# A linear-attention scan fused with a two-layer network: the first chunks' scores as whole 128-token products

## Chip, cores and metric

One NeuronCore of a Trainium2 chip. The metric is the device time of one execution in microseconds, from its start to its end on the slowest core (here the only one). Three executions of the kernel before were timed. One execution was also recorded by the hardware profiler; the rows below come from that one.

## The reference

For 4 batches, 8 heads, 768 tokens and 48 columns a head, all float32:

```
for t in range(768):
    cur = outer(u * k[t], v[t])
    y[t] = r[t] @ (state + cur)
    state = w[:, None] * state + outer(k[t], v[t])
h = x @ w_in                     x: 3072 tokens x 384 (the heads' y side by side), w_in: 384 x 2048
g = max(h, 0) + alpha * min(h, 0)
out = g @ w_out                  w_out: 2048 x 384
```

The decay w lies between 0.85 and 0.95 and differs by head and column.

## The kernel before, in words

**Chunks and pairs.** The tokens are cut into 6 chunks of L = 128. Heads go in P = 4 pairs: the first head of a pair lies in partitions 0 to 47, the second in 64 to 111, so that both use half of TensorE's rows. Within a chunk the scan becomes products: scores k'r between tokens (k and r scaled by powers of w from the tables W[q], made on VectorE), masked to earlier tokens, with u's share on the diagonal; then the scores times v; plus r times the state that came from earlier chunks.

**Chunk 0** is `first_chunk(q)`, lines 420 to 515, once for each pair. VectorE multiplies r and k by the tables (L431) and takes their product (L519). TensorE sums it with u (L526), ScalarE copies the sums to `cu` (L530). The scores are made in 64-token blocks: the two diagonal blocks (L445) and the cross block from early to late tokens (L449). `base` holds the diagonal blocks: first the identity times `cu` (ScalarE for the first heads, L462; VectorE for the second, L456), then VectorE writes the scores over it where the mask is set (L466). ScalarE copies the cross block to `off` (L470). `out` multiplies with v in two pieces (L480): the first 64 rows of the scores, then the last 64. ScalarE looks at one element between them (L486). The result is split in two parts of reduced precision (`xh`, `xl`: L392, L393, L395, and L381, L382 for the last pair), and some rows are moved by small transfers (L370). `state()` turns k to tokens by rows (`by_tokens`, L298: a product with `spread`, a diagonal matrix of w to the 64th; ScalarE copies it, L302) and multiplies by v (L508); ScalarE scales the result by w to the 64th (L513) into T[q].

**Later chunks** are made by `prepare` and `burst`, lines 537 to 679, pair by pair between the steps of the network, in 64-token halves, with the state handed from half to half (L664). Chunk 1 (`hasty`) also uses `by_tokens` and `diagonal`; from chunk 2 on k by tokens is loaded and scaled on VectorE, and u's sums are made on POOL.

**The network** runs in 96 steps of 128 hidden columns: `m_in` (L689, 9 matmuls: 3 blocks of rows by 3 products of split operands), an epilogue on ScalarE and VectorE (L697, L698, L701, L702), `m_out` (L722, 9 matmuls). Its order is chunk 0 steps 0 to 8, chunk 1 steps 0 to 8, the rest of chunk 0, the rest of chunk 1, then chunks 2 to 5. The weights of each of 16 steps are loaded once (L328) and split by ScalarE and VectorE (L346 to L357; L357, `wl`, is the last).

**What sets the order.** Every piece of work is added to a plan with an engine, an expected duration in us, what it reads and writes, and a rank. `in_order` (lines 95 to 175) runs a list schedule of these numbers; the pieces are issued in the order of their planned starts, so each engine's queue is fixed when the program is built. The first `m_in` has rank 0, by-token products of chunk 0 have rank -40 + q and come after the last product with v, and state products have rank 0.5 q + 0.2.

**Fillers.** `warm` (L233) is a bfloat16 matmul whose result nobody reads. 33 of them open the program; `with_warm` puts some in front of certain pieces, and line 819 to 822 put more into planned gaps of TensorE.

## Time and profile before

| | us |
|---|---|
| median of 3 executions | 505.71 |
| lowest, highest | 504.98, 506.17 |
| profiled execution, its own time | 506.03 |
| its span, first to last instruction | 504.3 |

Busy time of the engines over the span: TensorE 492.1, VectorE 310.8, ScalarE 243.1, POOL 41.9. The mean granted clock of TensorE is 0.975 of full speed. A busy TensorE counts overlapping matmuls once and takes modelled ends, so its share says that it always had something in it, not how fast it went; the granted clock says that. In groups of instructions, the mean duration of one is longer than the distance between two starts, since they overlap.

### The profile page before, as it was taken

What the parts mean: (1) busy time and instruction counts of PE and PEld (TensorE: products, weight loads), DVE (VectorE), ACT (ScalarE), POOL (GpSimd) and SP (SyncE); (2) the same over time, 40 slices, a digit from 0 to 9 for tenths busy, and PEclk for the clock granted to TensorE, in tenths of its full rate; (3) what the DMA queues carried; (4) which work ended last, traced back from release to release, by engine and by line L of the source; (5) the groups of instructions that cost most, each with busy time, mean ns of one, the idle gap of its engine ahead of it and who ended that gap; (6) DMA issues with size and microseconds to landing.
All of it is one profiled execution on the core that took longest, in us unless ns stands there. A gap on an engine that the chain in (4) does not pass through costs nothing.

```text
span 504.3 us, 11838 instructions
## 1 busy us (share of the span) xinstructions
PE 492.1 (98%) x4949; PEld 404.8 (80%) x4949; DVE 310.8 (62%) x522; ACT 243.1 (48%) x565; POOL 41.9 (8%) x48
## 2 busy tenths in 40 slices
PE   8899999899999999999999999999999999999994
PEld 6688888678888888888888888888888887888883
DVE  7553988999988668586476466667544534333331
ACT  4556578566765555355345355444443324422222
POOL 1000001000321101110122020121000000000000
PEclk9856999999999999999999999999999999999999
DMA  7436267646314363141221131312030000100001
GB/s 216 160 89 207 99 199 217 183 164 215 108 50 154 101 199 113 56 147 39 89 74 53 53 130 48 97 57 69 20 96 1 1 1 1 63 0 1 0 1 68
DMA packets 23739, 45.87 MB, mean 91 GB/s; under 512 B 3968, under 2 KB 11264, under 8 KB 23680
## 3 DMA queue, kind: packets, MB, share of 16 engines
q1 hardware_dynamic: 23680, 45.05, 28.6%
q8 instruction: 41, 0.67, 0.6%
q14 instruction: 18, 0.15, 0.1%
HBM read 36.38 MB, written 6.29 MB: 85 GB/s over the span
## 4 chain that ended last, share of the span: by engine, by line
PE 95%; DVE 2%; DMA 1%; issue 1%; SPq 0%; ACT 0%; ACTq 0%
PE bank L689 39%; PE acc L722 39%; PE bank L627 3%; PE bank L637 2%; PE bank L298 2%; PE bank L480 2%; PE bank L606 2%; PE bank L599 2%; PE acc L233 1%; DMA raw<-rk 1%; PE bank L508 1%; PE bank L393 1%; DVE raw L549 0%; PE acc L526 0%; PE bank L526 0%
## 5 line engine op out<-in xcount | busy, mean ns | idle before, releaser
L698 DVE SCALAR_TENSOR_TENSOR g<-bank,alph,g 128x512 f32<-128x512 f32 x96 | 71.9, 749 | 109.8 <-ACT g L697 109.5
L697 ACT ACTIVATE g<-bank 128x512 f32<-128x512 f32 x96 | 57.2, 596 | 141.7 <-PE bank L689 141.5
L689 PE MATMUL bank<-xh,wh 128*128 128x512 f32 x288 | 113.5, 394 | 0.0
L689 PE MATMUL bank<-xh,wl 128*128 128x512 f32 x288 | 112.3, 390 | 0.0
L689 PE MATMUL bank<-xl,wh 128*128 128x512 f32 x288 | 112.1, 389 | 0.0
L702 DVE TENSOR_TENSOR gl<-g,gh 128x512 fp32r<-128x512 f32 x96 | 70.6, 736 | 38.3 <-ACT gh L701 37.6
L701 ACT ACTIVATE gh<-g 128x512 fp32r<-128x512 f32 x96 | 60.5, 630 | 64.2 <-DVE g L698 64.1
L722 PE MATMUL acc<-gh,wh 128*128 128x512 f32 x288 | 83.6, 397 | 1.6 <-ACT gh L701 1.6
L722 PE MATMUL acc<-gl,wh 128*128 128x512 f32 x288 | 81.4, 390 | 0.2 <-DVE gl L702 0.2
L722 PE MATMUL acc<-gh,wl 128*128 128x512 f32 x288 | 81.6, 390 | 0.0
L722 PEld LDWEIGHTS acc<-gl,wh 128*128 128x128 f32 x288 | 53.9, 188 | 11.9 <-DVE gl L702 0.7
L722 PEld LDWEIGHTS acc<-gh,wh 128*128 128x128 f32 x288 | 52.5, 188 | 13.5 <-ACT gh L701 2.4
L689 PEld LDWEIGHTS bank<-xl,wh 128*128 128x128 f32 x288 | 54.2, 188 | 11.3
L689 PEld LDWEIGHTS bank<-xh,wh 128*128 128x128 f32 x288 | 54.2, 188 | 11.4
L722 PEld LDWEIGHTS acc<-gh,wl 128*128 128x128 f32 x288 | 54.0, 188 | 11.5
L689 PEld LDWEIGHTS bank<-xh,wl 128*128 128x128 f32 x288 | 54.2, 188 | 11.1
L560 POOL TENSOR_TENSOR rr<-rr,kk 128x384 f32<-128x384 f32 x16 | 19.8, 1236 | 306.6 <-DMA kk<-vkr 164.7
L571 ACT ACTIVATE base<-ident,cu 128x64 f32<-128x64 f32 x160 | 41.3, 337 | 1.9 <-DVE cu L566 1.8
L382 DVE TENSOR_TENSOR xl<-bank,xh 48x256 fp32r<-48x256 f32 (+1 forms) x66 | 28.4, 430 | 3.8 <-ACT xh L381 2.5
L381 ACT ACTIVATE xh<-bank 48x256 fp32r<-48x256 f32 (+1 forms) x66 | 25.4, 385 | 2.9 <-PE bank L637 1.0
L549 DVE TENSOR_TENSOR raw<-raw,W 112x512 f32<-112x512 f32 x40 | 26.3, 680 | 0.8 <-DMA raw<-rk 0.8
L562 POOL TENSOR_TENSOR rr<-rr,utab 128x384 f32<-128x384 f32 x16 | 19.8, 1239 | 1.3
(107 smaller groups left out, 421.9 us busy)
## 6 DMA issues: line engine op xcount, KB each, us to landing
wraw<-wall SPq DMA_DIRECT2D x16, 768.0 KB, 4.6
raw<-rk SPq DMA_DIRECT2D x46, 224.0 KB, 3.6
v<-vkr SPq DMA_DIRECT2D x24, 192.0 KB, 3.8
kk<-vkr SPq DMA_DIRECT2D x16, 192.0 KB, 3.3
rr<-vkr SPq DMA_DIRECT2D x16, 192.0 KB, 2.5
oT<-o SPq DMA_DIRECT2D x12, 256.0 KB, 2.2
oT<-g SPq DMA_DIRECT2D x6, 256.0 KB, 2.6
xh<-xh SPq DMA_DIRECT2D x36, 32.0 KB, 2.0
```

What stands on the lines that cost most here:

```text
L381: add("ACT", us, lambda: nc.scalar.activation(to(h), view(), AF.Copy), r=[src], w=refs(h), rank=rank)
L382: add("DVE", us + 0.1, lambda: nc.vector.tensor_tensor(out=to(l), in0=view(), in1=to(h), op=ALU.subtract), r=[src] + refs(h), w=refs(l), r ...
L549: add("DVE", 0.72, lambda t=t, tab=tab: nc.vector.tensor_tensor(out=t().rearrange("p b (j t) -> p (b j) t", j=2), in0=t().rearrange("p b ( ...
L560: add("POOL", 1.2, lambda: nc.gpsimd.tensor_tensor(out=rt(), in0=rt(), in1=k(), op=ALU.mult), r=[k] + ([wh[12]] if c == 2 else []), w=[rt] ...
L562: add("POOL", 1.2, lambda: nc.gpsimd.tensor_tensor(out=rt().rearrange("p (g b) e -> p g b e", g=2), in0=rt().rearrange("p (g b) e -> p g b ...
L571: add("ACT", 0.32, lambda g=g, b=b: nc.scalar.activation(base()[:, g, b], ident2(), AF.Copy, scale=cu()[:, g, b:b + 1]), r=[cu, ident2], w ...
L689: nc.tensor.matmul(hp()[:, :], a[i]()[:, k], x[c]()[:, k], start=(k == 0 and j == 0), stop=(k == NK - 1 and j == 2))
L697: add("ACT", 0.6, lambda: nc.scalar.activation(g(), hp()[:, :], AF.Copy), r=[hp], w=[g], rank=n - 100)
L698: add("DVE", 0.75, lambda: nc.vector.scalar_tensor_tensor(out=g(), in0=hp()[:, :], scalar=alph()[:, i:i + 1], in1=g(), op0=ALU.mult, op1=A ...
L701: add("ACT", 0.64, lambda: nc.scalar.activation(gh(), g(), AF.Copy), r=[g], w=[gh], rank=n - 100)
L702: add("DVE", 0.73, lambda: nc.vector.tensor_tensor(out=gl(), in0=g(), in1=gh(), op=ALU.subtract), r=[g, gh], w=[gl], rank=n - 99)
L722: nc.tensor.matmul(banks[k](), a[i]()[:, NK + k], x(), start=(begin and j == 0), stop=(end and j == 2))
```

## The change

Chunk 0: the scores of a head are one product of 128 by 128 tokens instead of three 64-token blocks. Each head's `base` is a tile of its own, whose diagonal is set by ScalarE for both heads, and whose scores VectorE writes under a full 128-token mask (`strict`, cast by POOL). The cross copy, VectorE's diagonal and ScalarE's look are gone. The product with v is one piece over all 128 tokens. `by_tokens` is four transposes and two copies without a scale; the state is scaled once, by w to the 128th (`w128`). Chunk 1 uses tables over 128 tokens too: its k by tokens is transposed, its state update adds without a scale, and ScalarE scales the state at its end. `warm` streams 384 columns instead of 256, with other counts, and the planner's expected durations are changed.

```diff
-BY_DVE = (1,)
+MM = 0.682
+WARM = 0.16
...
-    one, unit, ones = fixed([128, 2], "one"), sb([112, 65], "g", 3), sb([128, 128], "g", 3)
+    one, unit, ones = fixed([128, 2 + P], "one"), sb([112, 65], "g", 3), sb([128, 128], "g", 3)
...
-    spread = sb([112, P, 2, D], "rr", 1)
...
-        nc.tensor.matmul(into()[:, 256:512], x[:, 0:128], x, start=True, stop=True, skip_group_check=True)
+        nc.tensor.matmul(into()[:, 128:512].rearrange("p (a f) -> p a f", a=2), x[:, 0:128],
+                         x[:, None, 0:192].broadcast_to([128, 2, 192]), start=True, stop=True, skip_group_check=True)
 
     def with_warm(n, us, fn, r, w, rank):
 
-        p = add("PE", us + 0.107 * n, lambda: [warm(bank) for _ in range(n)] + [fn()], r=r + [ident] * (n > 0),
-            w=w + [(bank, ("warm", len(plan.pieces)))] * (n > 0), rank=rank)
+        p = add("PE", us + WARM * n, lambda: [warm(bank) for _ in range(n)] + [fn()], r=r + [ident] * (n > 0),
+                w=w + [(bank, ("warm", len(plan.pieces)))] * (n > 0), rank=rank)
         p.warm = n
+        return p
...
+    add("POOL", 0.3, lambda: nc.gpsimd.tensor_copy(strict(), ones()), r=[ones], w=[strict], rank=-60)
...
-    def spreads():
-
+    def small_tables():
         add("ACT", 0.3, lambda: nc.scalar.activation(minus(), ident()[0:112, 0:112], AF.Copy, scale=-1.0), r=[ident],
             w=[minus], rank=-60)
         for m in range(P):
-            add("ACT", 0.3, lambda m=m: nc.scalar.activation(
-                spread()[:, m], ident()[0:112].rearrange("p (g e) -> p g e", g=2)[:, :, 0:D], AF.Copy,
-                scale=W[m]()[:, L:L + 1]), r=[ident, W[m]], w=[(spread, m)], rank=-59 + m)
-
-    def by_tokens(q, k0, k, rank, behind=()):
+            add("ACT", 0.17, lambda m=m: nc.scalar.activation(
+                w128()[:, m:m + 1], W[m]()[:, L:L + 1], AF.Copy, scale=W[m]()[:, L:L + 1]), r=[W[m]], w=[(w128, m)],
+                rank=-39)
+
+    def by_tokens(k0, k, warms, rank, behind=()):
+
         t = psum()
 
-        def product():
+        def turn():
             for b in range(B):
-                nc.tensor.matmul(t()[:, 2 * D * b:2 * D * (b + 1)], k0()[:, b], spread()[:, q].rearrange("p g e -> p (g e)"),
-                                 start=True, stop=True, skip_group_check=True)
-
-        add("PE", 0.77, product, r=[k0, (spread, q)], w=[t], rank=rank).after.update(behind)
-        add("ACT", 0.5, lambda: nc.scalar.activation(
-            k().rearrange("p (g b) e -> p b g e", g=2),
-            t()[:, 0:2 * B * D].rearrange("p (b g e) -> p b g e", b=B, g=2), AF.Copy), r=[t], w=[k], rank=rank)
+                nc.tensor.transpose(t()[:, 112 * b:112 * (b + 1)], k0()[:, b], ident()[0:112, 0:112])
+
+        with_warm(warms, 0.5, turn, r=[k0, ident], w=[t], rank=rank).after.update(behind)
+        for g in range(2):
+            add("ACT", 0.3, lambda g=g: nc.scalar.activation(
+                k()[:, B * g:B * (g + 1)], t()[:, 0:448].rearrange("p (b x) -> p b x", b=B)[:, :, HI * g:HI * g + D],
+                AF.Copy), r=[t], w=[(k, g)], rank=rank)
...
-            for j in range(2):
-                add("ACT", 0.3, lambda m=m, j=j: nc.scalar.activation(
-                    rows()[:, m, HI * j:HI * (j + 1)], W[m]()[:, L - 1:HI - 1:-1], AF.Copy, scale=W[m]()[:, L:L + 1]), r=[W[m]],
-                    w=[(rows, (m, j))], rank=-21).after.update(last_out)
+            add("ACT", 0.36, lambda m=m: nc.scalar.activation(
+                rows()[:, m].rearrange("p (j t) -> p j t", j=2), W[m]()[:, None, L - 1:HI - 1:-1].broadcast_to([112, 2, HI]),
+                AF.Copy, scale=W[m]()[:, L:L + 1]), r=[W[m]], w=[(rows, m)], rank=-21).after.update(last_out)
...
-        lo, hi = slice(0, HI), slice(HI, L)
 
         def scores():
             for b in range(B):
-                at = slice(b * HI, (b + 1) * HI)
                 for g in range(2):
-                    for s in (lo, hi):
-                        nc.tensor.matmul(A[g]()[s, at], k0()[half(g), b, s], r()[half(g), b, s], start=(b == 0),
-                                         stop=(b == B - 1), skip_group_check=True)
+                    nc.tensor.matmul(A[g]()[:, b * L:(b + 1) * L], k0()[half(g), b], r()[half(g), b], start=(b == 0),
+                                     stop=(b == B - 1), skip_group_check=True)
+
+        with_warm(2, 1.05, scores, r=[r, k0], w=A, rank=q - 90)
+        base = [sb([128, B, L], "gl", 3, F32, mv) if q % 2 else sb([128, B, L], "base", 3) for _ in range(2)]
+        for g in range(2):
+            for b in range(B):
+                add("ACT", 0.39, lambda g=g, b=b: nc.scalar.activation(
+                    base[g]()[:, b], ident(), AF.Copy, scale=cu()[:, g, b:b + 1]), r=[cu, ident], w=[(base[g], b)],
+                    rank=-60 + q)
+        for g in range(2):
+            add("DVE", 0.73, lambda g=g: nc.vector.copy_predicated(
+                base[g](), strict()[:, None, :].broadcast_to([128, B, L]),
+                A[g]()[:, :].rearrange("p (b t) -> p b t", b=B)), r=[strict, A[g]], w=[base[g]],
+                rank=10 * q - 76 + g)
+        y = psum()
+
+        def out():
             for b in range(B):
                 for g in range(2):
-                    nc.tensor.matmul(A[g]()[lo, 256 + b * HI:256 + (b + 1) * HI], k0()[half(g), b, lo], r()[half(g), b, hi],
-                                     start=False, stop=(b == B - 1), skip_group_check=True)
-
-        with_warm(3, 0.95, scores, r=[r, k0], w=A, rank=q - 90)
-        base, off = sb([128, 2, B, HI], "base", 3), sb([128, 2, B, HI], "gl", 3, F32, mv)
-        for g in range(2):
-            if g in BY_DVE:
-                add("DVE", 0.42, lambda g=g: nc.vector.tensor_tensor(
-                    out=base()[:, g], in0=ident2()[:, None, :].broadcast_to([128, B, HI]),
-                    in1=cu()[:, g, :, None].broadcast_to([128, B, HI]), op=ALU.mult), r=[cu, ident2],
-                    w=[(base, (g, b)) for b in range(B)], rank=10 * q - 77 + g)
-                continue
-            for b in range(B):
-                add("ACT", 0.32, lambda g=g, b=b: nc.scalar.activation(
-                    base()[:, g, b], ident2(), AF.Copy, scale=cu()[:, g, b:b + 1]), r=[cu, ident2],
-                    w=[(base, (g, b))], rank=-60 + q)
-        for g in range(2):
-            add("DVE", 0.44, lambda g=g: nc.vector.copy_predicated(
-                base()[:, g], strict2()[:, None, :].broadcast_to([128, B, HI]),
-                A[g]()[:, 0:256].rearrange("p (b t) -> p b t", b=B)), r=[strict2, A[g]],
-                w=[(base, (g, b)) for b in range(B)], rank=10 * q - 76 + g)
-            add("ACT", 0.42, lambda g=g: nc.scalar.activation(
-                off()[lo, g].rearrange("p b t -> p (b t)"), A[g]()[lo, 256:512], AF.Copy), r=[A[g]], w=[(off, g)],
-                rank=-59.5 + q)
-        y = psum()
-
-        def out(rows, pieces):
-            for b in range(B):
-                for g in range(2):
-                    to, x = (lo if g == 0 else half(g)), g * B + b
-                    for n, (t, j) in enumerate(pieces):
-                        nc.tensor.matmul(y()[to, b * L + HI * j:b * L + HI * (j + 1)], v().rearrange("p x e -> p (x e)")[
-                            rows, x * D:x * D + to.stop - to.start], t()[rows, g, b], start=(rows == lo and b == n == 0),
-                            stop=(b == B - 1), skip_group_check=True)
-
-        with_warm(2, 0.78, lambda: out(lo, ((base, 0), (off, 1))), r=[v, base, off], w=[y], rank=q - 85)
-
-        add("ACT", 0.2, lambda: nc.scalar.activation(
-            seen_y()[:, 0:2], y()[HI:HI + 1, B * L - 2:B * L], AF.Copy), r=[y], rank=-99)
-        last_out[:] = [add("PE", 0.42, lambda: out(hi, ((base, 1),)), r=[v, base], w=[y], rank=q - 85.1)]
+                    rows, x = (slice(0, HI) if g == 0 else half(g)), g * B + b
+                    nc.tensor.matmul(y()[rows, b * L:(b + 1) * L], v().rearrange("p x e -> p (x e)")[
+                        :, x * D:x * D + rows.stop - rows.start], base[g]()[:, b], start=b == 0,
+                        stop=b == B - 1, skip_group_check=True)
+
+        last_out[:] = [with_warm(3, 0.95, out, r=[v] + base, w=[y], rank=q - 85)]
...
-            by_tokens(q, k0, k, -40 + q, last_out)
+            by_tokens(k0, k, 2, -40 + q, last_out)
...
-            add("PE", 0.47, product, r=[k, v], w=[U], rank=0.5 * q + 0.2)
+            add("PE", 0.75, product, r=[k, v], w=[U], rank=0.5 * q + 0.2)
             T[q] = sb([112, B, D], "T", 9)
-            add("ACT", 0.4, lambda t=T[q]: nc.scalar.activation(t(), u_rows(U, 0), AF.Copy, scale=W[q]()[:, L:L + 1]),
-                r=[U, W[q]], w=[T[q]], rank=0.5 * q + 0.2)
+            add("ACT", 0.4, lambda t=T[q]: nc.scalar.activation(t(), u_rows(U, 0), AF.Copy, scale=w128()[:, q:q + 1]),
+                r=[U, w128], w=[T[q]], rank=0.5 * q + 0.2)
...
-        with_warm(3 if mine != sums else 0, 0.45, c_sum, r=[prod, uw], w=[mine], rank=sum_rank)
+        with_warm(2 if mine != sums else 0, 0.56, c_sum, r=[prod, uw], w=[mine], rank=sum_rank)
...
+        span = L if hasty else HI
+        for t, tab in ((r, lambda: W[q]()[:, None, 0:span]), (k0, lambda: W[q]()[:, None, L - 1:(None if hasty else HI - 1):-1])):
             add("DVE", 0.72, lambda t=t, tab=tab: nc.vector.tensor_tensor(
-                out=t().rearrange("p b (j t) -> p (b j) t", j=2), in0=t().rearrange("p b (j t) -> p (b j) t", j=2),
-                in1=tab().broadcast_to([112, 2 * B, HI]), op=ALU.mult), r=[W[q]], w=[t], rank=at - 2)
+                out=t().rearrange("p b (j t) -> p (b j) t", t=span), in0=t().rearrange("p b (j t) -> p (b j) t", t=span),
+                in1=tab().broadcast_to([112, B * L // span, span]), op=ALU.mult), r=[W[q]], w=[t], rank=at - 2)
...
-            by_tokens(q, k0, k, at - 1.6)
+            by_tokens(k0, k, 0, at - 1.6)
...
-        first = add("PE", (0.7 if before else 0.1) + (0.8 if now else 0.1), run, r=uses, w=writes, rank=at)
+        us = {(1, 1): 3.0 if before and joint else 2.05, (1, 0): 1.8 if before and joint else 1.25, (0, 1): 1.5}
...
-            seen.soon[first] = 0.75
+            seen.soon[first] = 1.7 if joint else 1.05
...
-                    out=t(), in0=of(), scalar=W[q]()[:, L:L + 1], in1=u_rows(A[j], 256), op0=ALU.mult,
-                    op1=ALU.add), r=[A[j], T[q], W[q]], w=[t], rank=at - 0.4)
+                    out=t(), in0=of(), scalar=one()[0:112, 0:1] if c == 1 else W[q]()[:, L:L + 1], in1=u_rows(A[j], 256),
+                    op0=ALU.mult, op1=ALU.add), r=[A[j], T[q], W[q], (one, 0)], w=[t], rank=at - 0.4)
                 T1, T[q] = (t if j == 0 else T1), t
+            if c == 1:
+                add("ACT", 0.4, lambda t=t: nc.scalar.activation(t(), t(), AF.Copy, scale=w128()[:, q:q + 1]), r=[w128],
+                    w=[t], rank=at + 0.5)
...
-            add("PE", 0.7, mm, r=[wh[i], wl[i]] + [(t[c], (kx, p)) for t in (xh, xl) for kx in need for p in range(6)],
+            add("PE", MM, mm, r=[wh[i], wl[i]] + [(t[c], (kx, p)) for t in (xh, xl) for kx in need for p in range(6)],
...
-    add("PE", 7.0, lambda: [warm(bank) for _ in range(33)], r=[ident], w=[(bank, "warm")], rank=-1000)
+    add("PE", 6.7, lambda: [warm(bank) for _ in range(23)], r=[ident], w=[(bank, "warm")], rank=-1000)
...
-            begun = begun or p.rank >= 0 and p.us == 0.7
+            begun = begun or p.us == MM
             gap = 0.0 if last is None else max(0.0, p.start - last - 0.05)
-            if not begun or p.takes and gap > 0.3:
-                fill[p] = int(gap / 0.125), p.takes[0] if begun else bank
+            if gap > 0.25 and (not begun or p.takes):
+                fill[p] = int(gap / 0.17), p.takes[0] if begun else bank
```

The `m_out` pieces take `MM` in place of 0.7 as well, `spreads()` is called as `small_tables()`, and the spacer tile `space` goes.

## Rows read from the trace of the kernel before

**Rows 1.** The page: busy share of TensorE, and its granted clock in 40 slices.
```profile
PE 492.1 (98%) x4949; PEld 404.8 (80%) x4949; DVE 310.8 (62%) x522; ACT 243.1 (48%) x565; POOL 41.9 (8%) x48
...
PEclk9856999999999999999999999999999999999999
```

**Rows 2.** Windows: stretch and length, busy us (instructions) by engine, granted clock, DMA.
```profile
8.00:21.80 13.80, 12.30 (x328) 9.79 (x328) 10.20 (x24) 7.29 (x26) 0.00 (x0) 0.99 0.77 238
21.80:44.50 22.70, 22.70 (x239) 18.86 (x238) 8.18 (x14) 12.00 (x31) 0.00 (x0) 0.50 0.40 122
44.50:102.70 58.20, 56.40 (x783) 45.72 (x781) 51.16 (x81) 37.45 (x88) 2.04 (x2) 0.99 0.58 174
102.70:498.00 395.30, 395.17 (x3569) 326.24 (x3567) 236.40 (x392) 183.10 (x415) 37.55 (x30) 1.00 0.22 69
```

**Rows 3.** The chain of waits in order of time: start, us, what.
```profile
9.14 0.63 PE bank L445 x32
9.77 0.46 PE bank L449 x16
10.23 0.43 PE acc L233 x3
10.66 0.56 PE acc L526 x16
...
16.51 1.11 PE bank L480 x30
...
31.65 1.12 PE bank L393 x2
...
34.27 7.07 PE bank L298 x32
41.34 1.87 PE bank L508 x26
...
44.61 1.32 PE bank L689 x3
...
58.31 0.87 PE bank L298 x8
```

**Rows 4.** Windows of half a microsecond; the granted clock is the third number from the end.
```profile
21.50:22.00 0.50, 0.50 (x12) 0.28 (x7) 0.00 (x0) 0.00 (x0) 0.00 (x0) 0.60 0.00 0
...
45.50:46.00 0.50, 0.50 (x6) 0.37 (x4) 0.00 (x0) 0.50 (x3) 0.00 (x0) 1.00 0.85 167
```

**Rows 5.** Timeline of TensorE: start, us, line, tile, count, [idle before, releaser].
```profile
15.38 0.28 PE L445 MATMUL bank<-raw 48*64 48x64 f32 x3 [0.60 <-issue]
...
21.15 0.71 PE L480 MATMUL bank<-base,v 64*64 64x64 f32 x15 [0.82 <-issue]
```

**Rows 6.** Timeline of TensorE: three transposes and the matmul behind them.
```profile
45.77 0.45 PE L316 MATMUL bank<-ident,g 112*128 112x112 f32 x3
45.99 0.48 PE L689 MATMUL bank<-xh,wh 128*128 128x512 f32 x1
```

**Rows 7.** Groups of ScalarE from 9 to 44.5 us: busy us, mean ns of one.
```profile
L462 ACT ACTIVATE base<-ident,cu 128x64 f32<-128x64 f32 x16 | 4.4, 336 | 0.2
...
L302 ACT ACTIVATE kk<-bank 128x384 f32<-128x384 f32 x4 | 2.0, 490 | 3.9 <-PE bank L298 2.3 <-PE bank L508 1.6
...
L470 ACT ACTIVATE gl<-acc 64x256 f32<-64x256 f32 x4 | 1.3, 367 | 1.3 <-PE acc L449 1.3
```

**Rows 8.** Groups of VectorE from 4.6 to 44.5 us: busy us, mean ns of one.
```profile
L456 DVE TENSOR_TENSOR base<-ident,cu 128x256 f32<-128x256 f32 x4 | 1.7, 418 | 1.5 <-ACT cu L530 1.5
L466 DVE COPY_PREDICATED base<-strict,acc 128x256 f32<-128x256 uint8 x4 | 1.5, 438 | 1.6 <-ACT base L462 1.3 <-ACT gl L470 0.2
```

**Rows 9.** Timelines: the last of step 8's weights (VectorE), its first matmul (TensorE).
```profile
101.76 0.95 DVE L357 TENSOR_TENSOR wl<-wx,wh 128x768 fp32r<-128x768 f32 x1
...
102.69 0.40 PE L689 MATMUL bank<-xh,wh 128*128 128x512 f32 x1
```

More of the change, by code (lines that the diff above doesn't have):

```diff
@@ L310, in half_table @@
         for m in range(P):
[L311 to L314 removed]
+            add("ACT", 0.36, lambda m=m: nc.scalar.activation(
+                rows()[:, m].rearrange("p (j t) -> p j t", j=2), W[m]()[:, None, L - 1:HI - 1:-1].broadcast_to([112, 2, HI]),
+                AF.Copy, scale=W[m]()[:, L:L + 1]), r=[W[m]], w=[(rows, m)], rank=-21).after.update(last_out)
         for m in range(P):
[L316 removed]
+            add("PE", 0.12, lambda m=m: nc.tensor.transpose(
                 pt()[:, 128 * m:128 * m + 112], rows()[:, m], ident()[0:112, 0:112]),
[L318 removed]
+                r=[(rows, m), ident], w=[(pt, m)], rank=-20)
         add("DVE", 0.4, lambda: nc.vector.tensor_copy(
@@ L645, in run @@
                 products()
-        first = add("PE", (0.7 if before else 0.1) + (0.8 if now else 0.1), run, r=uses, w=writes, rank=at)
+        us = {(1, 1): 3.0 if before and joint else 2.05, (1, 0): 1.8 if before and joint else 1.25, (0, 1): 1.5}
+        first = add("PE", us[before is not None, now is not None], run, r=uses, w=writes, rank=at)
         if before:
-            row, col = (HI, L) if joint else (0, L)
+            row, col = (HI, 3 * L) if joint else (0, L)
             seen = add("ACT", 0.2, lambda: nc.scalar.activation(
                 seen_y()[:, 0:2], y[1]()[row:row + 1, col + HI - 1:col + HI + 1], AF.Copy), r=[y[1]], rank=at - 200)
-            seen.soon[first] = 0.75
+            seen.soon[first] = 1.7 if joint else 1.05
             add("PE", 0.3, lambda: through_scores(1), r=[v0, base0], w=y[joint:], rank=at - 200)
@@ L725, in m_out @@
             for k in range(NK):
-                add("PE", 0.7, lambda k=k: [mm(j, (k,)) for j in range(3)], r=[wh[i], wl[i], gh, gl], w=[banks[k]],
+                add("PE", MM, lambda k=k: [mm(j, (k,)) for j in range(3)], r=[wh[i], wl[i], gh, gl], w=[banks[k]],
                     rank=n + MLAG - 0.5)
@@ L729, in m_out @@
             for j in range(3):
-                add("PE", 0.7, lambda j=j: mm(j, range(NK)), r=[wh[i], wl[i], gl if j == 2 else gh], w=banks,
+                add("PE", MM, lambda j=j: mm(j, range(NK)), r=[wh[i], wl[i], gl if j == 2 else gh], w=banks,
                     rank=n + MLAG - 0.5)
```

7 lines of the change are left out of this document (2 added, 5 removed).

## The prediction

> **What bounds the kernel now.** I began with the page: busy shares, then its strip of 40 slices. TensorE is busy for 98% of the span, so time can only be won where TensorE works slowly or on something that need not be done. The strip of the granted clock shows the slow place: full speed everywhere but in slices 2 to 4 [rows 1]. Next came the busy time of each engine by stage [rows 2]. From 21.8 to 44.5 us TensorE is busy all of 22.7 us at a granted clock of 0.50, which is 1.2 GHz of its 2.4, while VectorE has 8.18 us of work and ScalarE 12.00. From 102.7 to 498 us TensorE idles 0.13 us in 395: nothing is to be had there but by removing matmuls. Between these two, from 44.5 to 102.7, TensorE idles 1.8 us and VectorE 7.0.
>
> The chain of waits in order of time says what fills the slow stage: the products with v (L480), the by-token products (L298, 7.07 us for the four pairs), the state products (L508), and then, at 44.61, the first matmul of the feed-forward part (L689) [rows 3]. All of it is TensorE's own queue, one piece after the other. The half-microsecond windows date the clock: it drops inside 21.5 to 22.0 and is back inside 45.5 to 46.0, just after the L689 matmuls start [rows 4]. Ahead of the drop the timeline shows two holes in TensorE that no engine explains, 0.60 and 0.82 us put down to issue, each in the middle of a run of equal matmuls [rows 5].
>
> So the target is one number: the start of the first L689, now 44.6 us. What comes behind it is TensorE bound and moves along with it, if the weights keep up.
>
> **The change on TensorE, pair by pair (four pairs), at the full clock.** Durations are from the chain [rows 3].
> - Scores. Removed: 0.63 + 0.46 = 1.09 us of 64-column products. Added: 8 products (16 instructions) of 128 columns, two row groups side by side. The nearest row has that pattern, the cross block L449: 16 instructions of 64 columns in 0.46; twice the columns gives 0.92. If nothing ran side by side, the price of L298 holds (0.87 / 8 for 96 columns, 0.145 for 128), 2.32 in all; if the four-way pattern of L445 held, 0.63. I take 0.92.
> - Product with v. Removed: 1.11 for the lower half and 0.71 for the upper [rows 3, 5]. Added: 16 instructions of 128 columns over both halves of the tokens. The lower half's row gives 0.037 for 64 columns, so 1.18 in all; the same upper bound of 2.32, lower 0.63.
> - k by tokens. Removed: 0.87. Added: 4 transposes. The trace has transposes in L316: three start at 45.77, and the matmul behind them starts at 45.99, about 0.073 each [rows 6]. Four: 0.30. Upper bound: their single durations end to end, 0.45 each at the worst, 1.8.
> - Filler matmuls. 8 of 256 columns at 0.143 become 9 of 384 columns, 0.215 each if time goes with columns: 1.15 becomes 1.94. The lower bound is that width costs nothing, 0.143 each, or 1.29.
>
> Before: 1.09 + 1.82 + 0.87 + 1.15 = 4.93. After: 0.92 + 1.18 + 0.30 + 1.94 = 4.34. That is 0.6 us a pair, 2.4 in all: small at the full clock. The rest depends on the clock.
>
> The queue up to the first L689 is then 4 x (0.56 for the diagonal sums + 4.34) = 19.6, three subtracting matmuls (L393, 1.12 for two at half clock, so 0.28 each) 0.8, and two state products (L508, 26 instructions in 1.87 at half clock, so 0.58 for 16) 1.2; less 0.4 for the first two fillers, which lie ahead of the first sums: 21.2 us. It starts, as before, when the first product of r and k is there, at about 8.1 us (the first transfers and VectorE's first three passes are untouched). **First L689 at 29.3, 15.3 us earlier.** The kernel of before at full clock would be there at 21.8 + 11.35 = 33.2, so about 11 of the 15 are the clock and 4 are removed work and holes: fewer, longer instructions should meet fewer holes like those of [rows 5].
>
> **Does the clock stay?** In the stage before the drop TensorE spent its time on 64-column products in quarters of the array, 2-column sums, and two holes. Afterwards the products are twice as wide, the filler streams half as many columns again, and planned gaps over 0.25 us are filled. I think it likelier than not that it holds, with no row that proves it.
>
> **ScalarE and VectorE in the same stage.** ScalarE's copies for the diagonal go from 16 of 64 columns to 32 of 128, 0.336 each for 64 [rows 7]; a 384-column copy takes 0.490, so about 0.36 each, some 0.28 apart when back to back: plus 5 us. Removed are the 8 evictions L470 (2.6) and four tiny L486 copies. By tokens it has 8 copies instead of 4, plus 1. From 8 to 44.5 it was busy 19.3 us [rows 2]; about 22 now, of which some 4 (later weights, the half table) can wait. That is 18 us in the 20 between the first sums and 29.3: it fits, with little to spare, and a delay there delays the splits that L689 needs. VectorE loses four L456 (0.418) and doubles the width of eight L466 (0.438) [rows 8]: plus 0.3 on 18.4, in 21 us. What does not fit is the preparation of the second weights, which slides past the first L689.
>
> **From the first L689 on.** Chunk 1's four by-token products save 4 x (0.87 - 0.30) = 2.3 us of TensorE. Its four extra ScalarE scalings of the state (about 0.4 each) have nobody waiting soon, and ScalarE has 20 idle us in that stage [rows 2]: nothing. Its powers over 128 tokens have the same number of elements: nothing. The mask that POOL now casts once more is first read after the first scores, long after POOL is done with its opening work, and the half table's eight copies become four of twice the width on a ScalarE that waits there: nothing for either, a few tenths if the cover went. But this stage runs at the pace of the weights: the last of VectorE's preparation for step 8 ends at 102.71 and that step's matmul starts at 102.69 [rows 9]. With 7.0 idle us of VectorE and up to 2.5 us of second-weight work slid in, I charge 2.3 against the gain (bounds: 0 to 5), so this stage nets zero (minus 2.3 to plus 2.7). The new planner prices (0.682 instead of 0.7 for three matmuls, larger ones for bursts) can reorder pieces; behind 102.7 there are 0.13 idle us to win, and I price that at zero (bounds minus 0.1 to plus 1.5, the size of the idle time already met in the middle stage).
>
> **Sum.** The profiled execution took 506.03 (span 504.3), 0.3 above the median of 505.71. 506.0 - 15.3 = 490.7; against the median **490.4 us**.
>
> **Rivals.**
> *The clock falls late all the same* (about 21.8, as before, or among the transposes). The rest of the queue costs double: at 21.8, 13.7 of 21.2 us are done and 7.5 become 15, first L689 at 36.8, total 498; a fall at 25 gives 494.5. For it: the diagonal sums stay, and transposes and state products are short. Against it: the wider products. The Trainium skill, TensorE: Matmul & The Clock Gate, Part 4 (PE-mode transpose), says that transposes do not count as busy work as matmuls do, and measures about 275 ns for one in a kernel; by that the by-token stage would be where the clock is lost, and the four would take an estimated 1.1 us. No run here shows a clock lost on transposes; L316's starts are closer together than that figure. Chance 0.18.
>
> *The weights hold the middle stage.* If VectorE loses its order as well as its slack, step 8 comes not 15 but 10 us earlier: total 495 to 496. For it: the row pair of [rows 9]. Against: 7 idle us. Chance 0.15.
>
> *Slower: the clock is lost in the first stage.* The start has 23 fillers instead of 33, the sums have 2 instead of 3, and ScalarE's longer copies make TensorE wait. Lost at 9 us, the queue is 0.9 + 2 x 20.3, first L689 at 49.6, total 511. It decides where 8.1 + x + 2 (21.2 - x) = 44.6, x = 5.9: a fall before 14.0 us is slower, one after it faster. Against it: through that stretch the clock of before held [rows 2], with less streamed. Chance 0.08.
>
> *Nothing measurable*: a fall very near 14 us, or several delays that add up to 15. Chance 0.03.
>
> **How the numbers follow.** The forecast has 0.56: 490.4, its own range 486 (fillers at their lower bound, the weights in time) to 494. The range 485 to 500 takes in the late fall and the late weights and leaves the early one out, together with products that do not run side by side (plus 8 to 10). A measurement of this kernel can tell about 0.2%, 1 us, from no change. Faster 0.89 (forecast, late fall, late weights), within 0.2% 0.03, slower 0.08.
>
> **What the profile will show.** Right: no 0.5 window between 20 and 45 us, first L689 between 27 and 32, 16 score instructions in about 0.9 us, transposes near 0.07 apart, the stage from first L689 to step 8 still near 58 us, and the stretch behind it unchanged at 395. Wrong: a half-clock stretch of over 5 us; ScalarE busy without a break to past 30 us with TensorE in fillers; score products at 0.145 an instruction; or step 8's weights at 95 us or later.

## The result and the profile after

The kernel after took 488.32 us in the median (487.33 to 494.74), the kernel before beside it 505.52 (504.98 to 506.17): a ratio of 0.9653, with a 95% interval from 0.9629 to 0.9676. The forecast was 490.4, with 485 to 500 as its range.

Either kernel can lose TensorE's full clock somewhere in its opening stage, the mean granted clock of an execution tells whether it did, and the ratio counts the four executions of before (all of which lost it, by their times) and those of after that kept it. Over all runs of this study the kernel before kept the clock (mean 0.996 or more) in 22 of 53 executions, 493.9 to 496.9 us with a median of 495.6, and lost it in 31, 503.0 to 507.7 with a median of 505.0 (0.969 to 0.979 in the 27 whose clock is on record; the four beside the result are counted by their times). The kernel after kept it in 8 of 9 executions, 487.2 to 491.8 with a median of 488.2, and lost it for long in one, 494.74. So the 17.2 us are two things: 9.9 us (505.5 to 495.6; 9.4 from the median of all 31) for a clock that before loses more often than not, and 7.4 us (495.6 to 488.2), 1.5%, for the kernel at the same clock.

The first profile of after is of that one execution. Its page, on the lines of [rows 1]:

```profile
span 493.0 us, 11246 instructions
PE 483.3 (98%) x4649; PEld 392.4 (80%) x4649; DVE 309.8 (63%) x518; ACT 247.2 (50%) x577; POOL 47.1 (10%) x49
PEclk9589999999999999999999999999999999999999
```

300 matmuls fewer, and a slow place again, but in another slice: earlier than in [rows 1], and shorter. The windows of one microsecond date it (the granted clock is the third number from the end):

```profile
11.00:12.00 1.00, 1.00 (x10) 0.43 (x10) 1.00 (x3) 1.00 (x5) 0.00 (x0) 0.55 1.06 339
...
28.00:29.00 1.00, 1.00 (x14) 0.69 (x14) 0.78 (x3) 0.37 (x1) 0.00 (x0) 0.92 0.11 20
```

The timeline of TensorE has a wait ahead of that fall: the first diagonal sums (L506, before: L526) come at 8.91 after 1.83 idle us, because an input landed late: VectorE waits 1.05 us for a transfer of r and k at 7.47. The first matmul of the network (L675, before: L689) starts at 36.75.

```profile
8.91 0.63 PE L506 MATMUL acc<-uw,g 112*64 112x2 f32 x16 [1.83 <-DVE g L499]
...
36.75 0.50 PE L675 MATMUL bank<-xh,wh 128*128 128x512 f32 x1
```

### The profile page after: what moved, and what is told of

It reads as the page before. It is cut to its first block, busy times and chain, and to the rows that moved or that the text cites. A ratio compares the mean times of both kernels' runs of the same rounds, so it can differ in the third digit from the quotient of the medians.

```text
span 493.0 us, 11246 instructions
## 1 busy us (share of the span) xinstructions
PE 483.3 (98%) x4649; PEld 392.4 (80%) x4649; DVE 309.8 (63%) x518; ACT 247.2 (50%) x577; POOL 47.1 (10%) x49
## 3 DMA queue, kind: packets, MB, share of 16 engines
q1 hardware_dynamic: 23680, 45.05, 29.3%
## 4 chain that ended last, share of the span: by engine, by line
PE 88%; DVE 5%; DMA 3%; ACT 2%; SPq 1%; issue 0%; DVEq 0%; ACTq 0%
PE acc L708 39%; PE bank L675 38%; PE bank L609 2%; DMA raw<-rk 2%; PE bank L619 2%; PE bank L588 2%; PE acc L232 2%; PE bank L581 1%; DMA wraw<-wall 1%; PE acc L443 1%; PE bank L464 1%; DVE raw L531 1%; DVE wx L354 1%; PE acc L506 1%; DVE wx L351 1%; PE bank L443 1%
## 5 line engine op out<-in xcount | busy, mean ns | idle before, releaser
L675 PE MATMUL bank<-xh,wh 128*128 128x512 f32 x288 | 113.3, 394 | 0.0
L675 PE MATMUL bank<-xh,wl 128*128 128x512 f32 x288 | 112.1, 389 | 0.0
L675 PE MATMUL bank<-xl,wh 128*128 128x512 f32 x288 | 112.1, 389 | 0.0
L688 DVE TENSOR_TENSOR gl<-g,gh 128x512 fp32r<-128x512 f32 x96 | 67.9, 707 | 40.9 <-ACT gh L687 40.0
L675 PEld LDWEIGHTS bank<-xl,wh 128*128 128x128 f32 x288 | 54.1, 188 | 11.4
L675 PEld LDWEIGHTS bank<-xh,wh 128*128 128x128 f32 x288 | 54.1, 188 | 11.3
L675 PEld LDWEIGHTS bank<-xh,wl 128*128 128x128 f32 x288 | 54.1, 188 | 10.8
L542 POOL TENSOR_TENSOR rr<-rr,kk 128x384 f32<-128x384 f32 x16 | 22.3, 1395 | 291.5 <-DMA kk<-vkr 214.7
L544 POOL TENSOR_TENSOR rr<-rr,utab 128x384 f32<-128x384 f32 x16 | 22.2, 1387 | 1.3
```

Source lines behind the costliest of these rows:

```text
L542: add("POOL", 1.2, lambda: nc.gpsimd.tensor_tensor(out=rt(), in0=rt(), in1=k(), op=ALU.mult), r=[k] + ([wh[12]] if c == 2 else []), w=[rt] ...
L544: add("POOL", 1.2, lambda: nc.gpsimd.tensor_tensor(out=rt().rearrange("p (g b) e -> p g b e", g=2), in0=rt().rearrange("p (g b) e -> p g b ...
L675: nc.tensor.matmul(hp()[:, :], a[i]()[:, k], x[c]()[:, k], start=(k == 0 and j == 0), stop=(k == NK - 1 and j == 2))
L688: add("DVE", 0.73, lambda: nc.vector.tensor_tensor(out=gl(), in0=g(), in1=gh(), op=ALU.subtract), r=[g, gh], w=[gl], rank=n - 99)
```

## Experiments

### The kernel after, once more

No edit.

> The changed kernel itself, once more, for a second trace. My theory: its first trace lost the clock at 11.4 us because the second pair of inputs came late (the diagonal sums waited 1.83 us), and most executions don't. Then this one keeps full clock past 12 us, has its first feed-forward matmul at 29 to 31 us instead of 36.75, and takes 487 to 489. Rival: the clock is always lost at about 11 us, and the difference lies elsewhere: a half-clock stretch of over 10 us again, first matmul after 35 us.

Measured: 488.59 us (487.15 to 491.77); the traced execution took 487.15. Its page and its windows by stage, to be held against [rows 1, 2]:

```profile
span 485.4 us, 11246 instructions
PE 475.8 (98%) x4649; PEld 387.7 (80%) x4649; DVE 310.4 (64%) x518; ACT 247.1 (51%) x577; POOL 48.0 (10%) x49
PEclk9999999999999999999999999999999999999998
```

```profile
7.50:28.51 21.01, 20.28 (x248) 14.28 (x248) 17.73 (x33) 17.44 (x51) 0.00 (x0) 1.00 0.60 178
28.51:84.10 55.59, 53.90 (x808) 43.71 (x806) 52.37 (x85) 43.27 (x106) 6.66 (x2) 1.00 0.73 229
84.10:479.00 394.90, 394.90 (x3569) 326.36 (x3568) 236.06 (x391) 182.33 (x413) 38.73 (x30) 1.00 0.22 69
```

The clock is whole, and the first network matmul starts at 28.51. The stage from there to the last of step 8's weights is 55.6 us where it was 58.2 [rows 2]; what follows is 394.9 where it was 395.3. But that boundary has moved: the last of these weights is now ready 0.87 us ahead of the matmul that follows. To that matmul itself the stage is 56.5 us (28.51 to 84.98) where it was 58.1 (44.54 to 102.69), 1.7 less.

```profile
83.16 0.95 DVE L358 TENSOR_TENSOR wl<-wx,wh 128x768 fp32r<-128x768 f32 x1
...
84.98 0.39 PE L675 MATMUL bank<-xh,wh 128*128 128x512 f32 x1
```

The timeline of TensorE prices the new pieces:

```profile
8.23 0.63 PE L506 MATMUL acc<-uw,g 112*64 112x2 f32 x16 [1.16 <-DVE g L499]
...
9.23 1.16 PE L443 MATMUL bank<-raw 48*128 48x128 f32 x16
10.32 0.50 PE L232 MATMUL acc<-ident 128*128 128x384 bf16 x2
10.75 0.63 PE L506 MATMUL acc<-uw,g 112*64 112x2 f32 x16
...
15.36 0.66 PE L232 MATMUL acc<-ident 128*128 128x384 bf16 x3
15.95 1.09 PE L464 MATMUL bank<-base,v 128*64 128x128 f32 x16
16.97 0.50 PE L232 MATMUL acc<-ident 128*128 128x384 bf16 x2
...
26.02 0.55 PE L300 MATMUL bank<-ident,raw 112*128 112x112 f32 x4
26.40 0.49 PE L232 MATMUL acc<-ident 128*128 128x384 bf16 x2
26.73 0.55 PE L300 MATMUL bank<-ident,raw 112*128 112x112 f32 x4
...
28.16 0.55 PE L300 MATMUL bank<-ident,o 112*128 112x112 f32 x4
28.51 0.50 PE L675 MATMUL bank<-xh,wh 128*128 128x512 f32 x1
...
31.83 1.13 PE L488 MATMUL bank<-v,kk 128*64 128x48 f32 x32
```

From start to start: scores 10.32 - 9.23 = 1.09, the product with v 1.02, four transposes 0.38, a filler 0.43 / 2 = 0.215 (0.59 / 3 ahead of the product with v, 0.33 / 2 ahead of the transposes).

From the first sums (8.23) to the first network matmul TensorE has no wait left: 20.28 us. That stretch is 20.27 to 20.38 in the five traces of the kernel after and its variants that keep the clock and have this opening queue (this one, 31 fillers, chunk 1 as before, the first weights earlier, the old durations), while the sums start anywhere from 7.91 to 9.54 us. So TensorE's own queue, with the fillers planned into its gaps, sets the first network matmul, and a difference of up to 1.6 us in its start between two such traces is the start of the sums.

### The fillers alone, and all but the fillers

The kernel before with the new fillers:

```diff
-        nc.tensor.matmul(into()[:, 256:512], x[:, 0:128], x, ...)
+        nc.tensor.matmul(into()[:, 128:512].rearrange("p (a f) -> p a f", a=2), x[:, 0:128],
+                         x[:, None, 0:192].broadcast_to([128, 2, 192]), ...)
...
-            if not begun or p.takes and gap > 0.3:
-                fill[p] = int(gap / 0.125), p.takes[0] if begun else bank
+            if gap > 0.25 and (not begun or p.takes):
+                fill[p] = int(gap / 0.17), p.takes[0] if begun else bank
```

> The kernel before with the fillers of the change alone (384 columns, 2, 2 and 3 of them ahead of the pieces, 23 at the start, gaps over 0.25 us filled). Theory that 11 of the 15 us are the clock and that the fillers keep it: no half-clock stretch, first feed-forward matmul at 32 to 35, time 494 to 497. Rival, that the wide products keep it: the clock still falls near 22 us, the time stays within 1.5 of 505.5.

Measured: 497.7 us (496.43 to 498.39), all eight executions at 0.995 or more; ratio to the executions of before that kept the clock 1.0045 (1.0032 to 1.0058). The first network matmul stood at 31.64. The clock is kept, as the first theory has it (its time a little above the 494 to 497 expected), and against the kernel before at full clock nothing is won: 2 us are lost, with 33 fillers in planned gaps after the network's start, where the trace has only 0.65 idle us ahead of them.

The kernel after with the old fillers (the same edit backwards, with the counts of before):

> The changed kernel with the fillers of before (256 columns, 3, 3 and 2, none ahead of the transposes, 33 at the start). Theory that the fillers keep the clock: it falls between 15 and 28 us, first feed-forward matmul at 33 to 38, time 492 to 498. Rival, that the wide products keep it by themselves: no half-clock stretch, 2 to 4 us less of filler, time 484 to 489.

Measured: 493.65 us (491.70 to 495.73) in ten executions at 0.988 or more. The rival is right about the clock of the opening stage: the wide products keep it by themselves. The time is some 5 us above the kernel after, not below it as the rival had it; it lies in the theory's range, but not for the theory's reason. In the traced execution (494.67) the first sums start at 8.03 and the first network matmul comes at 29.92, a stretch 1.6 us longer than the kernel after's; from there to the last matmul it takes 456.0 us against 451.2. Some 1.7 of these 4.8 are the half of 3.4 us at half clock, from 73.0 on. Most of the rest is in waits of TensorE that the kernel after does not have:

```profile
PE bank L618 <- ACT seen_y L633: 3.2, 3, 1.4
...
PE acc L707 <- ACT gh L686: 0.9, 1, 0.9
```

The four executions at 0.998 or more took 492.1 to 493.9 us, so the old fillers cost about 4.5 us with the clock kept. Planned durations changed with the fillers, the list schedule ordered the queues anew, and three times TensorE stands before the second half of a product whose release comes late. This trace also has sixteen transposes behind one another (L299, starting 0.10 us apart, the fourth operand's at 26.52), and the windows around them at full clock:

```profile
25.37 1.31 PE L299 MATMUL bank<-ident,raw 112*128 112x112 f32 x12
26.52 0.55 PE L299 MATMUL bank<-ident,o 112*128 112x112 f32 x4
```

```profile
24.00:26.00 2.00, 2.00 (x25) 1.73 (x25) 1.75 (x6) 1.94 (x4) 0.00 (x0) 1.00 0.15 33
26.00:28.00 2.00, 1.72 (x18) 1.39 (x15) 1.30 (x3) 1.93 (x5) 0.00 (x0) 1.00 0.25 57
```

### Chunk 1 as before, and no transposes at all

The kernel after with chunk 1's k by tokens as a product again:

```diff
-        span = L if hasty else HI
+        span = HI
...
-            by_tokens(k0, k, 0, at - 1.6)
+            by_product(q, k0, k, at - 1.6)
...
-                    out=t(), in0=of(), scalar=one()[0:112, 0:1] if c == 1 else W[q]()[:, L:L + 1], in1=u_rows(A[j], 256),
+                    out=t(), in0=of(), scalar=W[q]()[:, L:L + 1], in1=u_rows(A[j], 256),
```

> The changed kernel with chunk 1 as before (64-token powers, k by tokens as a product with w to the 64th, the state scaled at each half, no scaling by ScalarE). Theory of the forecast, that the stage runs at the pace of the weights: within 1 us of the changed kernel. Rival, that TensorE bounds that stage: 2 to 3 us slower than the changed kernel (4 x 0.57).

Measured: 490.8 us (489.64 to 491.77), 2.2 above the kernel after beside it. The rival is right: chunk 1's way of before costs about what TensorE saves by the transposes. In the trace all of it lies behind the first network matmul, 453.6 us to the last one against 451.2; 0.7 of these 2.4 is idle time of TensorE (2.1 us in that stretch against 1.4), since the queue's order changed with the edit. Step 8's weights were ready at 82.42, 1.7 us earlier than in the kernel after, and the end came later all the same.

The same in chunk 0 too, without fillers ahead of them:

```diff
-            by_tokens(k0, k, 2, -40 + q, last_out)
+            by_product(q, k0, k, -40 + q, last_out)
```

> The changed kernel with k by tokens made by products with w to the 64th in chunk 0 and chunk 1 (and the state scaled by w to the 64th at each half), without fillers ahead of them in chunk 0. The fourth experiment had this in chunk 1 alone and took 490.8. Theory that ScalarE and the first weights set the first feed-forward matmul, so that chunk 0's transposes give nothing: within 0.8 of that, 490 to 491.6. Rival, that TensorE sets it: first matmul 1 to 2.2 us later, 491.8 to 493.

Measured: 490.69 us (490.15 to 492.47). Within 0.8 of the one above: chunk 0's transposes, with their fillers, give nothing that shows in the time. The traces show what they give. The first network matmul was 1.2 us later (29.45 against 28.28); 0.6 of that is a later start of the first sums (8.52 against 7.91), and 0.6 the longer queue from the sums on (20.94 against 20.38). Nothing of it was made up in the network: from there to the last matmul (481.89, and 483.08 without transposes) both take 453.6 us.

```profile
7.91 0.63 PE L523 MATMUL acc<-uw,g 112*64 112x2 f32 x16 [0.50 <-DVE g L516]
```

```profile
8.52 0.63 PE L523 MATMUL acc<-uw,g 112*64 112x2 f32 x16 [0.85 <-DVE g L516]
```

What hides it lies behind the start of the last matmul, where the outputs leave: 7.2 us in the first of these traces and 5.8 in the second. In the three traces of the kernel before, unchanged, that end takes 5.9 to 6.8 us, so a gain of 0.6 can't be read from a few times.

### The first weights earlier

The kernel after with ScalarE's passes on the first weights at a rank 20 lower:

```diff
-rank=need - 3 - 42 * (i == 0)
+rank=need - 3 - 62 * (i == 0)
```

> The changed kernel with ScalarE's two passes on the first step's weights ranked ahead of the diagonals (rank 20 lower). Theory that these weights are what the first feed-forward matmul waits for (ready at 28.05, matmul at 28.51): it comes 0.5 to 1.5 us earlier, 487 to 488. Rival, that the diagonals, delayed by 1.7 us, then hold the products with v: the same or up to 1.5 us later.

Measured: 489.2 us (488.80 to 490.78), not faster. VectorE's last pass on these weights starts at 25.37 instead of 27.10, and the first network matmul comes at 29.34 instead of 28.51, behind the transposes as before. The difference is the start of the first sums (9.01 against 8.23); from there it takes 20.33 us against 20.28, with the weights ready 3 us ahead. So it was not the weights that it waited for, but TensorE's own queue.

### The opening: fewer and more fillers

The kernel after with 13 fillers at the start:

```diff
-    add("PE", 6.7, lambda: [warm(bank) for _ in range(23)], ...)
+    add("PE", 6.7, lambda: [warm(bank) for _ in range(13)], ...)
```

> The changed kernel with 13 instead of 23 fillers at the start, planned time untouched: TensorE then idles some 3 us ahead of the first sums instead of 1.2. Theory that a hole there is what loses the clock early: half clock from 9 to 12 us on in nearly every execution, first feed-forward matmul at 35 to 38, time 494 to 497. Rival, that the hole does not matter: 487 to 489 as the changed kernel.

Measured: 495.12 us (493.15 to 496.08), all four executions at 0.983 to 0.986, first network matmul at 32.56, ahead of the 35 to 38 expected, since the clock came back on the way. The windows show the fall and the return:

```profile
8.00:10.00 2.00, 2.00 (x34) 1.54 (x32) 1.45 (x3) 1.07 (x5) 0.00 (x0) 1.00 0.92 290
10.00:12.00 2.00, 2.00 (x20) 1.07 (x18) 1.88 (x4) 1.25 (x5) 0.00 (x0) 0.52 1.06 289
...
20.00:22.00 2.00, 2.00 (x34) 1.51 (x31) 0.69 (x2) 0.87 (x3) 0.00 (x0) 0.92 0.00 0
22.00:24.00 2.00, 2.00 (x25) 1.30 (x21) 0.73 (x1) 1.50 (x7) 0.00 (x0) 1.00 0.00 0
```

```profile
1.48 4.98 PE L232 MATMUL acc<-ident 128*128 128x384 bf16 x15 [1.48 <-POOL ident L260]
7.79 0.63 PE L506 MATMUL acc<-uw,g 112*64 112x2 f32 x16 [1.33 <-DVE g L499]
```

The clock is lost early each time, as expected, but not by the hole I meant to make. The fillers run at 0.33 us each here, so the wait came out at 1.33 us, hardly longer than the 1.16 of the kernel after when it kept its clock. What is smaller is the work ahead of it. Whether that or the slightly longer wait loses the clock, no run separates.

The kernel after with 31 fillers:

> The changed kernel with 31 instead of 23 fillers at the start, planned time untouched, which closes the hole ahead of the first sums. Theory: no execution loses the clock early (none of 494), and the fillers overrun by 0.1 to 0.5 us: 487.5 to 489.5 throughout. Rival, that late inputs lose the clock all the same: one in five at 492 to 495.

Measured: 488.91 us (488.57 to 489.82), ratio 0.9872 (0.9855 to 0.9889), all four at 0.996 or more. The first network matmul is at 29.81, since the fillers overrun. It is the evenest version of all, and no faster in the median; four executions can't show that it never loses the clock.

### The planner's durations

The kernel after with the durations of before:

```diff
-MM = 0.682
+MM = 0.7
...
-        us = {(1, 1): 3.0 if before and joint else 2.05, (1, 0): 1.8 if before and joint else 1.25, (0, 1): 1.5}
+        us = {(1, 1): 1.5, (1, 0): 0.8, (0, 1): 0.9}
```

> The changed kernel with the planner's durations of before (0.7 for three matmuls, 1.5, 0.8 and 0.9 for bursts, 0.75 until the result is looked at, 0.47 for the state product). Forecast: within 1.5 us of the changed kernel. Rival, that the new durations are what keeps TensorE without holes from the first feed-forward matmul on: 2 to 6 us slower, with idle time of TensorE or fillers between 30 and 100 us.

Measured: 489.81, 490.29 and 491.67 us where the clock was kept (and 499.42 in one that lost it). About 2 us above the kernel after: the rival, at its lower end. In the trace they lie behind the first network matmul, 453.7 us to the last one against 451.2. TensorE's waits for the network's epilogue add up to 2.0 us, of which the kernel after has none; but it has 1.4 us of other waits there, so idle time accounts for less than 1 us, and what the rest is stays open:

```profile
PE acc L708 <- ACT gh L687: 2.0, 4, 0.9
```

### Where the kernel before loses its clock

Unchanged, twice, for a trace at full clock:

> The kernel before itself, for a trace at full clock. In the runs beside the first four experiments it took 494.8 to 496.5 in ten executions and 503.0 to 506.4 in eight. Theory: the shorter times are those that keep the clock; then the first feed-forward matmul is at 33 to 34 us (21.8 + 22.7 / 2 = 33.2), and the rest of the program takes 460 as in the trace of before. Rival: the rest differs too: first matmul after 36, rest under 458.

> The kernel before again, for the trace that the fifth experiment missed: of an execution that keeps the clock. Theory: the hole of 0.8 to 1.2 us at the 348th matmul, ahead of the fall in both traces so far, is absent or shorter than 0.5 us in it; first feed-forward matmul at 33 to 34, the rest 460 us. Rival: the same hole stands there and the clock holds all the same, so that the hole alone does not decide.

Both missed: each traced execution had lost the clock (503.47 and 503.51 us; first network matmul at 42.89 and 43.34, rest of the span 458.8 and 458.4). Whether an execution of before that keeps the clock has the hole was therefore not seen. Both traces again have the hole of [rows 5] at the same place, after the first of L480's sixteen; here the later one:

```profile
20.02 0.27 PE L480 MATMUL bank<-base,v 64*64 64x64 f32 x1
20.92 0.65 PE L480 MATMUL bank<-base,v 64*64 64x64 f32 x15 [0.63 <-issue]
```

Counted from the program's start, that first one is the 348th matmul, in all three traces. The earlier hole of [rows 5], which only the first trace has, stands after the 221st. So the kernel before got eight more fillers at the start:

```diff
-    add("PE", 7.0, lambda: [warm(bank) for _ in range(33)], ...)
+    add("PE", 7.0, lambda: [warm(bank) for _ in range(41)], ...)
```

> The kernel before with 41 instead of 33 fillers at the start, planned time untouched: the hole ahead of the first sums is closed, everything behind it is as before. Theory: the late fall of the clock comes from the hole inside the stage, at the 348th matmul (three traces have it there), so it stays: part of the executions at 503 to 507, part at 495 to 497, and the hole, if a disturbed execution is recorded, again behind the 348th matmul, eight matmuls earlier in the program (in the sums of the last pair). Rival, that the hole ahead of the first sums decides, as in the changed kernel: all executions at 495 to 497.

Measured: 505.52 us (503.07 to 509.22), all six executions at 0.968 to 0.979, while the kernel before beside it kept the clock in five of twelve. The expected share of executions at 495 to 497 did not come; at before's own rate (31 of 53) six out of six would lose it by chance about once in 25 times. The hole has moved by exactly eight matmuls, into the sums of the last pair, again after the 348th, and in this trace it is longer:

```profile
19.06 0.45 PE L526 MATMUL acc<-uw,g 112*64 112x2 f32 x9
21.67 0.40 PE L526 MATMUL acc<-uw,g 112*64 112x2 f32 x7 [2.16 <-issue]
```

```profile
20.00:22.00 2.00, 0.33 (x7) 0.31 (x7) 0.56 (x1) 0.13 (x1) 0.00 (x0) 1.00 0.00 0
22.00:24.00 2.00, 2.00 (x34) 1.47 (x34) 0.47 (x2) 0.68 (x3) 0.00 (x0) 0.62 0.04 8
```

The hole goes with a count of instructions, not with a piece of work, and the clock falls 0.5 to 2.2 us behind its end in the four traces. The count alone does not make it: the kernel before with the new fillers has no hole at its 348th matmul, the second of three fillers, and kept its clock.

```profile
20.16 0.68 PE L481 MATMUL bank<-base,v 64*64 64x64 f32 x16
20.77 0.66 PE L233 MATMUL acc<-ident 128*128 128x384 bf16 x3
```

That the hole is a wait for the next instructions is a reading: 127 matmuls with their weight loads are 254 instructions, and TensorE's 9898 over the 41 packets of the page's instruction queue (q8) make 241 each. The traces' packets of that queue fit it. One starts at 18.66 us in the first trace of before, at 18.38 and 18.61 in the next two and at 19.21 with 41 fillers, takes 1.1 us, and TensorE goes on 1.2 to 1.4 us behind its end each time (21.15, 20.78, 20.92, 21.67). With the new fillers that packet starts at 18.28, and TensorE needs 5.3 us from the 222nd matmul to the 348th instead of 4.4 to 4.7, so it gets there at 20.9, when by the same lag the instructions are in. No run moved the packet alone, so the cause stays a reading, and so does the step from the hole to the fall of the clock: no trace has the hole and a clock that holds, but none separates the hole from the width of the fillers either. The kernel after reaches its 348th matmul only behind the network's start, and its traces have no such hole in the opening stage.

## Why the prediction was right, point by point

**The target.** It named the start of the first network matmul and forecast 29.3; at full clock it was 28.5 in one trace of the kernel after, and TensorE's queue sets it, as forecast. The sum per pair held as well: 1.09 for the scores against 0.92, 1.02 against 1.18 for the product with v, 0.38 against 0.30 for the transposes, 1.78 for nine fillers (0.43 + 0.43 + 0.59 + 0.33) against 1.94. Together this is 4.27 against 4.34. The score term was low because 0.46 was the share of the chain: from start to start those sixteen matmuls take 0.57 in the same trace (9.59 to 10.16 below), and twice that is 1.14. One term did not happen: the two state products (1.2 us) that the sum puts ahead of the first network matmul stand behind it in the kernel after (L488, from 31.83), where before has three of its four ahead. Without them the sum gives 28.1, so 29.3 was near partly by luck.

```profile
9.59 0.64 PE L449 MATMUL bank<-raw 48*64 48x64 f32 x16
10.16 0.50 PE L233 MATMUL acc<-ident 128*128 128x256 bf16 x3
```

**The clock.** Forecast: 11 of 15 us are the clock, from half of the slow stage. Between executions of before that lose and keep it lie 9.4 to 9.9. What the step did not see is that one trace cannot show how often the clock falls. That all four executions of before beside the result lost it was luck, about one chance in nine at 31 of 53; had they kept it, the same change would have been worth 7.4 us, half of the 15 forecast. The reason given, wider products, more filler and fewer holes, divides like this: the wide products alone keep the clock in the opening stage, the fillers alone keep it too, and the traced executions of before lose it just behind the hole of [rows 5]. That fewer, longer instructions avoid such holes stood in the forecast as a remark beside the sum; no traced execution that keeps the clock has a hole of that size in its opening stage.

**Transposes and the clock.** The rule from the Trainium skill that was weighed there (TensorE: Matmul & The Clock Gate, Part 4) would lose the clock in the by-token stage. Sixteen transposes behind one another, starting 0.10 us apart, with the clock at 1.00 in the windows that hold them, do not bear it out here; but they last 1.3 us, and no run has a longer stretch of them. Its 275 ns agrees with the trace as the duration of one, 262 ns; since they overlap, four cost 0.38 us and not the 1.1 that the rival worked out:

```profile
L300 PE MATMUL bank<-ident,raw 112*128 112x112 f32 x28 | 3.9, 262 | 0.9 <-DVE raw L531 0.9
```

**From the first network matmul on.** This step failed. I let the weights hold that stage and charged 2.3 us against chunk 1's transposes, for a net of zero. The runs keep most of the 2.3: 2.2 us are lost when chunk 1 goes back to products, and from the first network matmul to the last the kernel after takes 450.6 to 451.2 us where before takes 452.5 to 452.9, although it took in three more state products (an estimated 1.7 us, from the forecast's 0.58 each). Step 8's matmul close behind its weights [rows 9] was no wait for them: TensorE's waits in that stage of before are for the network's epilogue (1.6 us for `gh`, 0.2 for `gl`), and with chunk 1 as before the weights came 1.7 us earlier while the time grew. The term of the planner's durations was mis-sized: at most 1.5 was allowed, about 2 measured.

**ScalarE and VectorE.** ScalarE's wide copies measured 0.390 each against 0.36, and VectorE's wide writes 0.71 to 0.73 against 0.68:

```profile
L450 ACT ACTIVATE base<-ident,cu 128x128 f32<-128x128 f32 x16 | 5.2, 390 | 0.9 <-PE bank L464 0.8
```

It fitted, with little to spare, as forecast: ScalarE was busy for 17.4 of the 21.0 us up to the first network matmul.

**The rivals.** The early fall happened, in one of nine executions, at 11.1 us (0.55 of full clock in the microsecond from 11). By the forecast's formula a fall before 14.0 makes the kernel slower than before; it took 494.74. The formula let the half clock last to the network's start, and here it was back at 28.2, in the run with 13 fillers at about 20, both among the wide products. The step that failed is that price, not the mechanism. The late fall was not seen in the kernel after, though one of four executions with the old durations, 499.42 us, lost its clock at a place that no trace shows.

**Left open.** What an execution of before looks like that keeps its clock, and with it whether the hole is what loses it; and what of the 7.4 us at the same clock lies ahead of the first network matmul. An estimate is 5 to 6, since behind it only 1.3 to 2.3 are won; the forecast had 4 ahead and none behind.

## What to carry to other kernels

A stage at half clock in one trace can be one throw of a die: run the same kernel a dozen times and sort the times by their mean granted clock before pricing what a change does to it. Where TensorE stops in the middle of equal matmuls with nothing to wait for, count its instructions from the start: fewer and longer ones can move or remove the hole, while fillers added ahead only shift it. In a queue ordered by planned durations, those are part of the kernel: old fillers cost about 4.5 us and old durations 2 us with the clock kept. And before a difference of 1 us between two traces is explained, subtract where the first sums start and what the outputs take at the end, since both vary by about 1 us from execution to execution.

## What the runs showed of the hardware that was not expected

TensorE's hole stood behind the 348th matmul in all three traces of the kernel before and in that with eight more fillers, 0.63 to 2.16 us long, and moved with the count when they were added; with the new fillers it was not there. The first fillers of a program run at half the pace of later ones although the view reads a clock of 1.00 there. In the second trace of the kernel after they start 0.32 us apart up to 4.3 us and 0.16 from there on:

```profile
1.48 5.60 PE L232 MATMUL acc<-ident 128*128 128x384 bf16 x25 [1.48 <-POOL ident L260]
```

The change comes where that trace's record of the clock begins, so the 1.00 ahead of it is no measurement. And the clock came back inside the opening stage after some 10 us (13 fillers) and 17 us (the kernel after), while in the kernel before it stayed down for 20 to 24 us, until the network's matmuls.
